# All weights of attention's part staged in the second batch's x memory in slots 0 to 9, and five buffers for v

## The chip, the cores and the metric

The kernel runs on one core of a Trainium2 chip. The metric is the device time of one execution in microseconds (us), median over the runs. The engines of the core work side by side: TensorE (PE, the matmuls, with PEld for its weight loads), VectorE (DVE), ScalarE (ACT), GpSimd (POOL) and SyncE (SP), which here issues every DMA.

## What is computed

Three stages follow each other, all in float32. Attention has 4 batches of 8 heads, 576 positions and 64 columns a head, with a decay term and a causal mask; its output is the input x (2304 tokens, 512 columns) of a first MLP, and that of a second one.

```python
scores = scale * np.matmul(q, k.transpose(0, 1, 3, 2))
cum = np.cumsum(np.log(np.clip(f, 0.0001, 1.0)), axis=-1)
scores = np.where(causal, -1e9, scores + cum[..., :, None] - cum[..., None, :])
attn = softmax(scores)                  # written out in the reference
x = np.matmul(attn, v)                  # then (2304, 512)
h = x @ w_in                            # 512 -> 2048, first MLP
g = np.maximum(h, 0) + alpha * np.minimum(h, 0)
x = g @ w_out                           # 2048 -> 512
out = ((x @ w_a) * (x @ w_b)) @ w_out2  # 512 -> 1536 -> 512, second MLP
```

## The kernel before

Attention goes head by head in 32 slots plus a tail. In slot u PE computes the scores of head u, ACT exponentiates them (line 394), and two slots later `pv` (lines 504 to 520) multiplies the exponentials with v. The exponentials of a head come in three parts, PT_hi, PT_lo and PT_r. Heads 0, 1, 4, 5, 8 and 9 go in whole float32: PE transposes them, and `eng0` in the table `_P` says which engine copies the transposed tile out of PSUM (e4 is the copy of PT_r; lines 249 on ACT, 251 on DVE). The other heads are split into a rounded and a rest part, p_hi, p_lo and p_r (DVE at line 496, POOL at 445), and DMAs transpose them (line 502). For those heads v is split as well: `split_v` (line 347) runs two POOL operations on it. `load_v` (line 338) brings v; before the change there are three v buffers, head u+1 is loaded in slot u, and a buffer is free when `pv` of the head three before it is done. Two finished heads are normalized (xn, xr, lines 532 and 534) and turned by PE (tx, line 548) into the hidden layout, xh and xl (lines 552 and 553), two float32 halves of x.

Beside the slots the first MLP is fed to PE in small portions. It uses 7 blocks of 128 of its 2048 hidden columns in this stage (F1A = 7), so 7 weights of w_in and 7 of w_out, 512 KB each. `fetch` (line 133, on SP) loads a weight, `rounded` splits it by bit arithmetic (ACT at 142, DVE at 144, 145 and 146), and `parts` writes the two halves (ACT at 150, POOL at 151). `ws` in `_P` lists in which slot each of the 14 weights is rounded. `mlp1a` (line 650) computes h with three matmuls for each product (`mm3`, lines 643 to 645), then `leaky`: lu on ACT (637), lt on DVE (638), g on ACT (639), the rest of g on POOL (640); then y, copied by ACT (ys, 685) and stored by SP (686). It starts in slot 10; from that slot on the MLP's matmuls fill the gaps of attention's. Attention's last slot ends at about 365 us; after that come the rest of the first MLP (from 365 on the two kernels have the same code) and the second MLP.

A scheduler orders the instructions of each engine when the kernel is built, and each engine then runs its row of instructions strictly in that order: an instruction that waits holds everything behind it on its engine.

Memory before: while the first MLP has not begun, weights go through a pool `early` with two raw buffers (wr, 4 KB a partition) and one for the rounding (wx); when the MLP begins that pool is closed, and a pool `wstage` with one raw buffer and one wx takes the last three weights, in slots 10 and 11. x has two buffers each for xh and xl, one a batch in turn; the second batch's are first written in slot 11.

Of the kernel before, what the change touches and what calls it, by code (L numbers as in the profile page):

```python
# [10 lines left out]
I32 = mybir.dt.int32  # L11
# [7 lines left out]
B, H, S, D = 4, 8, 576, 64  # L19
# [3 lines left out]
C = DM // 128  # L23
# [21 lines left out]
    rates=[0, 1, 1, 1, 0.8, 1.15, 1.15, 0.95],  # L45
    ws=[0, 1, 2, 3, 4, 5, 6, 7, 8, 9, 9, 10, 10, 11],
    native=10,
    pre=1,
    we=0,
    es=10,  # L50
    eng0={'e0': 'act', 'e2': 'act', 'e3': 'dve', 'e4': 'dve'},
    even0='s3 T p1 s2 vs s0 Q M M M M h3 h2 h0 h1 l1 l2 p0 s1 l0 l3 ri p2 V W M'.split(),
# [37 lines left out]
def decay_attention_then_two_mlps(ctx, tc, q, k, v, f, w_in, w_out, alpha, w_a, w_b, w_o, out):  # L90
# [39 lines left out]
    def fetch(kind, i):  # L130

        raw = mp["stage"].tile([128, C, 128, 2], I32, tag="wraw", name=f"wr_{kind}{i}", bufs=mp["wraw"])
        sp.dma_start(raw.rearrange("p c e t -> p c (e t)"), w_src[kind](i))
        return raw

    def rounded(kind, i, after):

        raw = raws.pop((kind, i), None) or fetch(kind, i)
        low, high = raw[:, :, :, 0], raw[:, :, :, 1]
        x = mp["stage"].tile([128, C, 128], I32, tag="wx", name=f"wx_{kind}{i}", bufs=mp.get("wx"))  # L140
        with tc.issue_after(after) if after is not None else nullcontext():
# [119 lines left out]
    def attention_setup():  # L261
# [35 lines left out]
        for nm in ("nmr", "smr"):  # L297
            ap_[nm] = a.tile([128, 2], F32, tag=nm, name=nm)
        for i in range(3):

            ap_["vs", i] = a.tile([128, 3, NQ, D], F32, tag=f"vs_{i}", name=f"vs_{i}")
            zeros(ap_["vs", i][SR:, :, 4])
# [32 lines left out]
    def load_v(n):  # L335
        b, h = divmod(n, H)
        vs = ap_["vs", n % 3]
        sp.dma_start(vs[:, 0, 0:4], v[b, h, 0:ST].rearrange("(t p) d -> p t d", p=128))
        sp.dma_start(vs[0:SR, 0, 4], v[b, h, ST:])

    def split_v(n):

        if whole(n):
            return
        vs = ap_["vs", n % 3]
        for i in range(2):
            pool.tensor_tensor(vs[:, i + 1], vs[:, i], high(vs[:, i]), op=ALU.subtract)  # L347
# [156 lines left out]
    def pv(u, c):  # L504

        g, j = divmod(u, 2)
        vs = ap_["vs", u % 3]
        if u not in ps_x:
# [67 lines left out]
    def attention():  # L576

        cur = lambda u: 0 <= u < NI
        if LAG == 2:
            load_v(0)  # L580
        warm_up(_P.get("wu", [0, 0])[0], "a")
        stack(0)
# [5 lines left out]
        for u in range(NI + LAG):  # L588
            ap_["u"] = u
            for op in order(u):  # L590
# [28 lines left out]
                elif op == "V":  # L619
                    if cur(u + 3 - LAG):  # L620
                        load_v(u + 3 - LAG)
                elif op == "vs":
# [76 lines left out]
    if True:  # L699
        w1 = lpool(left, "w1", 2 * F1A)  # L700
        xpool = lpool(mid, "x", 2)
        early = ExitStack()
        ap_["early"] = mp["stage"] = lpool(early, "early", 1)
        mp["wraw"] = 2
        decay = decay_sums()
# [31 lines left out]
        def advance():  # L737
            if "g" not in mp:
                assert not raws
                early.close()  # L740
                mp["g"] = [lpool(mid, "g", 1)]
                mp["t"] = lpool(mid, "t", 2)
                mp["stage"] = lpool(mid, "wstage", 1)
                mp["wraw"] = 1
                scores_set(lpool(right, "att3", 1, "right"), 2)
# [10 lines left out]
        for kind, u in att:  # L756
            if kind == "W":
                if u == _P.get("dc", -1):
                    next(decay)
                if u < 0:  # L760
                    raws[todo[0]] = fetch(*todo[0])
                for m in range(_P["ws"].count(u), 0, -1):
                    with tc.high_priority(offset=-_P.get("wp", 0)):
                        if "g" not in mp and (m > 1 or u < NATIVE - 1):
                            raws[todo[1]] = fetch(*todo[1])
                        weight(*todo.pop(0), w1)
                continue
# [15 lines left out]
        mp["stage"] = lpool(right, "wstage2", 2, "right")  # L783
        mp["wx"], mp["wraw"] = 3, 2
        xp = lpool(right, "xb", 2, "right")
# [287 lines left out]
```

## Time and profile before

| | us |
|---|---|
| median of 3 runs (1066.59 to 1068.86) | 1068.8 |
| profiled execution | 1068.39 |
| its span in the trace | 1066.6 |
| around the span | 1.8 |
| PE busy in the span | 1014.8 |
| DVE, ACT, POOL busy in the span | 705.0, 457.4, 413.9 |

The profile page gives the busy time of each engine and the chain of work that ended last. A busy PE is not PE at its full clock: each stretch also has the clock that was granted, as a share of full speed (0.985 over the whole execution). So time is lost in two ways that are read apart, PE's idle time and PE's busy time at a granted clock under 1.

### The profile page before, as it was taken

Reading aid. Unit: us, or ns where it says so; the run is one execution under the profiler, and the core shown is the slowest. Engines: PE = TensorE matmul, PEld = TensorE weight load, DVE = VectorE, ACT = ScalarE, POOL = GpSimd, SP = SyncE. Lnnn points to the kernel's source line nnn. Section 1 sums busy time; section 2 is a strip of 40 time slices with the busy share of each in tenths; the row PEclk is TensorE's granted clock in tenths of the full one; section 3 lists DMA queues with packets and bytes.
Section 4 is the critical chain, followed back from the end, with each engine's and each line's share of the span. In section 5 each row is a group of like instructions: output and inputs, shape, how many; then the busy total and the mean of one; then the engine's idle time right before and its main releaser. Section 6 shows DMA issues by size and latency. Waiting matters only on the chain.

```text
span 1066.6 us, 20175 instructions
## 1 busy us (share of the span) xinstructions
PE 1014.8 (95%) x7485; PEld 959.2 (90%) x7485; DVE 705.0 (66%) x1461; ACT 457.4 (43%) x1035; POOL 413.9 (39%) x413
## 2 busy tenths in 40 slices
PE   5889799998989999999999998999999999999998
PEld 3678689998989999999999998899989999899997
DVE  6889877858767356444456658755986658975553
ACT  4676668758756354333343443322432113221110
POOL 4332623224224155333446866522443224531111
PEclk9999799999989999999999999999999999999999
DMA  6988768977886576756567996726328383353623
GB/s 151 196 190 225 175 142 158 217 159 164 188 194 110 160 246 197 231 190 210 179 231 251 342 366 255 297 96 238 106 93 313 116 315 122 120 209 135 247 89 109
DMA packets 206710, 206.14 MB, mean 193 GB/s; under 512 B 117076, under 2 KB 173908, under 8 KB 206612
## 3 DMA queue, kind: packets, MB, share of 16 engines
q1 hardware_dynamic: 206612, 204.85, 65.2%
q8 instruction: 59, 0.97, 0.4%
q14 instruction: 39, 0.32, 0.1%
HBM read 133.32 MB, written 50.17 MB: 172 GB/s over the span
## 4 chain that ended last, share of the span: by engine, by line
PE 75%; DVE 10%; DMA 6%; issue 3%; POOL 3%; ACT 2%; SPq 0%; POOLq 0%; DVEq 0%; ACTq 0%
PE p L643 7%; PE p L645 7%; PE p L644 7%; PE pv L520 4%; PE o L645 4%; PE o L643 4%; PE o L644 4%; PE ya L643 3%; PE hb L643 3%; PE ya L644 3%; PE hb L645 3%; PE hb L644 3%; PE ya L645 3%; PE y L644 2%; PE y L643 2%
## 5 line engine op out<-in xcount | busy, mean ns | idle before, releaser
L643 PE MATMUL p<-yq,w_h 128*128 128x384 f32 x360 | 121.8, 338 | 2.3 <-DVE lu L1019 1.3
L645 PE MATMUL p<-yq,w_h 128*128 128x384 f32 x360 | 121.3, 337 | 0.0
L644 PE MATMUL p<-yq,w_h 128*128 128x384 f32 x360 | 121.2, 337 | 0.0
L347 POOL TENSOR_TENSOR vs<-vs 128x320 f32<-128x320 f32 x52 | 44.6, 857 | 152.0 <-DMA vs<-in_v 121.2
L394 ACT ACTIVATE s<-s,nm 128x512 f32<-128x512 f32 (+3 forms) x128 | 71.4, 559 | 38.3 <-DVE nm L393 37.1
L643 PE MATMUL o<-w_o,gg 128*128 128x512 f32 x216 | 84.7, 393 | 1.7 <-ACT gg L1000 1.7
L644 PE MATMUL o<-w_o,gg 128*128 128x512 f32 x216 | 84.8, 393 | 0.0
L645 PE MATMUL o<-w_o,gg 128*128 128x512 f32 x216 | 83.2, 393 | 0.0
L1001 POOL TENSOR_TENSOR gg<-tc,gg 128x384 fp32r<-128x384 f32 x36 | 36.6, 1017 | 114.5 <-ACT gg L1000 97.3
L640 POOL TENSOR_TENSOR g<-lt,g 128x288 fp32r<-128x288 f32 x56 | 54.8, 985 | 62.7 <-ACT g L639 62.5
L640 POOL TENSOR_TENSOR gb<-lt,gb 128x384 fp32r<-128x384 f32 x54 | 55.7, 1031 | 59.2 <-ACT gb L639 58.0
L643 PE MATMUL h<-xh,w_in 128*128 128x288 f32 x224 | 67.6, 306 | 8.8 <-DVE lt L638 7.2
L644 PE MATMUL y<-g,w_out 128*128 128x288 f32 x224 | 67.7, 306 | 6.6 <-POOL g L640 6.6
L643 PEld LDWEIGHTS p<-yq,w_h 128*128 128x128 f32 x360 | 67.6, 188 | 6.9 <-DVE lu L1019 1.7
L1001 POOL TENSOR_TENSOR gg<-td,gg 128x384 fp32r<-128x384 f32 x36 | 38.0, 1056 | 89.7 <-ACT gg L1000 83.9
L644 PE MATMUL ya<-gb,w_out 128*128 128x384 f32 x216 | 72.7, 337 | 0.0
L645 PE MATMUL ya<-gb,w_out 128*128 128x384 f32 x216 | 72.5, 336 | 0.0
L643 PE MATMUL ya<-gb,w_out 128*128 128x384 f32 x216 | 71.1, 337 | 1.2 <-DVE yl L842 1.2
L1000 ACT CAST gg<-tc 128x384 fp32r<-128x384 f32 x36 | 18.5, 514 | 125.2 <-DVE tc L999 125.2
L638 DVE SCALAR_TENSOR_TENSOR lt<-lu,nal,hb 128x384 f32<-128x384 f32 x54 | 33.0, 611 | 57.9 <-ACT lu L637 57.9
L644 PEld LDWEIGHTS p<-yq,w_h 128*128 128x128 f32 x360 | 67.6, 188 | 3.7
L643 PE MATMUL y<-g,w_out 128*128 128x288 f32 x224 | 67.6, 312 | 2.8 <-ACT ys L685 2.4
(196 smaller groups left out, 3121.9 us busy)
## 6 DMA issues: line engine op xcount, KB each, us to landing
yq<-yq_d SPq DMA_DIRECT2D x49, 768.0 KB
yq_d<-yhl SPq DMA_DIRECT2D x42, 384.0 KB
yl<-ya_d SPq DMA_DIRECT2D x48, 192.0 KB
po_d<-os SPq DMA_DIRECT2D x36, 256.0 KB
os<-po_d SPq DMA_DIRECT2D x36, 256.0 KB
wr_in<-in_moe_w_in SPq DMA_DIRECT2D x16, 512.0 KB
wr_out<-in_moe_w_out SPq DMA_DIRECT2D x16, 512.0 KB
RK<-in_k SPq DMA_DIRECT2D x44, 144.0 KB
```

The costliest lines, as they stand in the source:

```text
L347: pool.tensor_tensor(vs[:, i + 1], vs[:, i], high(vs[:, i]), op=ALU.subtract)
L394: act.activation(s, s, AF.Exp, bias=nm, scale=-1.0, accum_out=sm)
L520: pe.matmul(o, p, high(vs[:, i, t]), start=start and x == 0, stop=stop and x == len(parts) - 1)
L638: dve.scalar_tensor_tensor(t, u, nal[:, fi:fi + 1], hp[:, :n], op0=ALU.mult, op1=ALU.add)
L640: pool.tensor_tensor(gl, t, f32(gh), op=ALU.subtract)
L643: pe.matmul(o, lh, rh, start=start, stop=False)
L644: pe.matmul(o, lh, rl, start=False, stop=False)
L645: pe.matmul(o, ll, rh, start=False, stop=stop)
L1000: ap_["last"] = act.copy(g[:, 0], o).ins
L1001: pool.tensor_tensor(g[:, 1], o, f32(g[:, 0]), op=ALU.subtract)
```

## The change

`ws` puts all 14 roundings into slots 0 to 9. Their memory comes from the xh and xl tiles of one of x's two buffers, taken under the names home_xh and home_xl: three raw buffers (two in home_xh, one in home_xl) and two for the rounding (in home_xl), used in turn. The first batch of x then takes the other buffer, and the second batch gets this one. Weights are fetched two ahead instead of one. `wstage` is gone. v has five buffers, and slot u loads the v of head u+2 (two loads stand at the start). Six copies of PT_r (`eng0`, e4) go from DVE to ACT.

```diff
-    ws=[0, 1, 2, 3, 4, 5, 6, 7, 8, 9, 9, 10, 10, 11],
+    ws=[0, 1, 1, 2, 3, 3, 4, 5, 5, 6, 7, 7, 8, 9],
-    eng0={'e0': 'act', 'e2': 'act', 'e3': 'dve', 'e4': 'dve'},
+    eng0={'e0': 'act', 'e2': 'act', 'e3': 'dve', 'e4': 'act'},
...
-        raw = mp["stage"].tile([128, C, 128, 2], I32, tag="wraw", name=f"wr_{kind}{i}", bufs=mp["wraw"])
+            raw = mp["home"].pop(0)
+            mp["home"].append(raw)
...
+            x = mp["homex"].pop(0)
+            mp["homex"].append(x)
...
-        for i in range(3):
+        for i in range(5):
             ap_["vs", i] = a.tile([128, 3, NQ, D], F32, tag=f"vs_{i}", name=f"vs_{i}")
...
-        vs = ap_["vs", n % 3]
+        vs = ap_["vs", n % 5]
...
             load_v(0)
+            load_v(1)
...
-                    if cur(u + 3 - LAG):
-                        load_v(u + 3 - LAG)
+                    if cur(u + 4 - LAG):
+                        load_v(u + 4 - LAG)
...
-        mp["wraw"] = 2
+        home = [xpool.tile([128, C * S], I32, tag=x, name=f"home_{x}") for x in ("xh", "xl")]
+        raw_, wx_ = 2 * C * 128, C * 128
+        mp["home"] = [
+            home[j][:, o:o + raw_].rearrange("p (c e t) -> p c e t", c=C, t=2) for j, o in ((0, 0), (0, raw_), (1, 0))
+        ]
+        mp["homex"] = [home[1][:, o:o + wx_].rearrange("p (c e) -> p c e", c=C) for o in (raw_, raw_ + wx_)]
...
-                mp["stage"] = lpool(mid, "wstage", 1)
-                mp["wraw"] = 1
...
-                    raws[todo[0]] = fetch(*todo[0])
-                for m in range(_P["ws"].count(u), 0, -1):
+                    for x in todo[:2]:
+                        raws[x] = fetch(*x)
+                for _ in range(_P["ws"].count(u)):
                     with tc.high_priority(offset=-_P.get("wp", 0)):
-                        if "g" not in mp and (m > 1 or u < NATIVE - 1):
+                        weight(*todo.pop(0), w1)
+                        if len(todo) > 1:
                             raws[todo[1]] = fetch(*todo[1])
-                        weight(*todo.pop(0), w1)
```

Line numbers of the changed kernel are 8 to 12 higher. What it moves is shown at three places.

**Slots 10 and 11, POOL and DVE.** First POOL before. vs_180, vs_176 and vs_178 are the v buffers (of heads 11, 12 and 10 here), g_0 is the first MLP block, w_out are weights, p_11_r is the part p_r of head 11.

```order
L151 TENSOR_TENSOR w_out_1044<-wx_out_1039,w_out_1044 128x512
L151 TENSOR_TENSOR w_out_1194<-wx_out_1189,w_out_1194 128x512
L347 TENSOR_TENSOR vs_180<-vs_180 128x320 x2
L445 TENSOR_SCALAR p_11_r<-sr 128x5x128
L151 TENSOR_TENSOR w_out_1202<-wx_out_1197,w_out_1202 128x512
L347 TENSOR_TENSOR vs_176<-vs_176 128x320 x2
L640 TENSOR_TENSOR g_0_1257<-lt_1280,g_0_1257 128x288
L640 TENSOR_TENSOR g_0_1257<-lt_1318,g_0_1257 128x288
L640 TENSOR_TENSOR g_0_1257<-lt_1369,g_0_1257 128x288
L640 TENSOR_TENSOR g_0_1257<-lt_1428,g_0_1257 128x288
L151 TENSOR_TENSOR w_out_1395<-wx_out_1390,w_out_1395 128x512
```

The same place on POOL in the changed kernel (vs_182, vs_184 and vs_186 are the further buffers, of heads 12, 13 and 14):

```order
L159 TENSOR_TENSOR w_out_929<-home_xl,w_out_929 128x512
L355 TENSOR_TENSOR vs_180<-vs_180 128x320 x2
L159 TENSOR_TENSOR w_out_1065<-home_xl,w_out_1065 128x512
L355 TENSOR_TENSOR vs_182<-vs_182 128x320 x2
L159 TENSOR_TENSOR w_out_1212<-home_xl,w_out_1212 128x512
L649 TENSOR_TENSOR g_0_1264<-lt_1287,g_0_1264 128x288
L649 TENSOR_TENSOR g_0_1264<-lt_1325,g_0_1264 128x288
L649 TENSOR_TENSOR g_0_1264<-lt_1376,g_0_1264 128x288
L649 TENSOR_TENSOR g_0_1264<-lt_1415,g_0_1264 128x288
L453 TENSOR_SCALAR p_11_r<-sr 128x5x128
L355 TENSOR_TENSOR vs_184<-vs_184 128x320 x2
L649 TENSOR_TENSOR g_0_1264<-lt_1463,g_0_1264 128x288
```

The last weights now stand ahead of the first g, the split of head 12 too, and p_11_r stands behind four of the g.

DVE before, around the first lt, the operation that feeds the first g:

```order
L393 ISA nm_164 128x1
L416 TENSOR_SCALAR smr<-smr 128x1
L496 SCALAR_TENSOR_TENSOR p_11_r<-sr,p_11_r 128x5x128
L496 SCALAR_TENSOR_TENSOR p_11_hi<-s_163,p_11_hi 128x7x128
L417 RECIPROCAL rir_167<-smr 128x1
L416 TENSOR_SCALAR sm_165<-sm_165 128x4
L553 TENSOR_TENSOR xl_1573<-tx_0_1574,xh_1572 128x256
L417 RECIPROCAL ri_166<-sm_165 128x4
L553 TENSOR_TENSOR xl_1573<-tx_1_1579,xh_1572 128x320
L496 SCALAR_TENSOR_TENSOR p_11_lo<-s_163,p_11_lo 128x3x128
L638 SCALAR_TENSOR_TENSOR lt_1280<-lu_1281,nal,h_0_0_1258 128x288
L638 SCALAR_TENSOR_TENSOR lt_1318<-lu_1319,nal,h_0_1_1286 128x288
```

And in the changed kernel:

```order
L401 ISA s_152,nm_153<-sc_3_1312,maskz 128x512
L401 ISA nm_153 128x1
L647 SCALAR_TENSOR_TENSOR lt_1287<-lu_1288,nal,h_0_0_1265 128x288
L647 SCALAR_TENSOR_TENSOR lt_1325<-lu_1326,nal,h_0_1_1293 128x288
L401 ISA s_152,nm_153<-sc_1_1346,maskz 128x256
L401 ISA nm_153 128x1
L259 COPY PT_9_lo<-tp_0_0_1352 128x384
L504 SCALAR_TENSOR_TENSOR p_10_hi<-s_152,p_10_hi 128x7x128
L424 TENSOR_SCALAR sm_154<-sm_154 128x4
L647 SCALAR_TENSOR_TENSOR lt_1376<-lu_1377,nal,h_0_2_1331 128x288
L504 SCALAR_TENSOR_TENSOR p_10_lo<-s_152,p_10_lo 128x3x128
```

The first lt stood behind the rest scores and p_11 of head 11; it now stands among the work of heads 9 and 10.

**Heads 6 and 7, SP.** Weight loads (L133, in the change L137), transposes (L502, in the change L510), v loads (L338, in the change L346) and the other loads share this one row. Before:

```order
L502 DMA_TRANSPOSE PT_hi<-p_6_hi 128x14x128
L502 DMA_TRANSPOSE PT_lo<-p_6_lo 128x6x128
L338 DMA vs_180<-in_v 128x4x64
L339 DMA vs_180<-in_v 64x64
L502 DMA_TRANSPOSE PT_r<-p_7_r 128x10x128
L133 DMA wr_out_899<-in_moe_w_out 128x1024
L502 DMA_TRANSPOSE PT_hi<-p_7_hi 128x14x128
L502 DMA_TRANSPOSE PT_lo<-p_7_lo 128x6x128
L338 DMA vs_176<-in_v 128x4x64
L339 DMA vs_176<-in_v 64x64
```

In the changed kernel, the same heads:

```order
L137 DMA home_xh<-in_moe_w_out 128x1024
L332 DMA RK_150<-in_k 64x576
L334 DMA RQ_149<-in_q 64x576
L510 DMA_TRANSPOSE PT_hi<-p_6_hi 128x14x128
L346 DMA vs_178<-in_v 128x4x64
L347 DMA vs_178<-in_v 64x64
L137 DMA home_xh<-in_moe_w_out 128x1024
L332 DMA RK_163<-in_k 64x576
L510 DMA_TRANSPOSE PT_lo<-p_6_lo 128x6x128
L336 DMA RQ_162<-in_q 64x512
L510 DMA_TRANSPOSE PT_r<-p_7_r 128x10x128
L510 DMA_TRANSPOSE PT_hi<-p_7_hi 128x14x128
```

The weight load stands ahead of PT_hi of head 6 and again ahead of PT_lo, where it stood between PT_r and PT_hi of head 7; the v load of a head stands one head earlier against the transposes.

**The start, ACT.** The first weight's rounding (wx_in, in the change home_xl) beside the work of head 0. Before:

```order
L394 ACTIVATE s_150,sm_152<-s_150,nm_151 128x256
L249 COPY PT_0_hi<-tp_2_0_248 128x384
L413 ACTIVATE sr,smr<-sr,nmr 128x576
L142 ACTIVATE wx_in_229<-wr_in_207 128x512
L394 ACTIVATE s_163,sm_165<-s_163,nm_164 128x512
L249 COPY PT_0_lo<-tp_0_0_269 128x384
```

In the changed kernel:

```order
L402 ACTIVATE s_152,sm_154<-s_152,nm_153 128x256
L150 ACTIVATE home_xl<-home_xh 128x512
L257 COPY PT_0_hi<-tp_2_0_254 128x384
L421 ACTIVATE sr,smr<-sr,nmr 128x576
L150 ACTIVATE home_xl<-home_xh 128x512
L402 ACTIVATE s_165,sm_167<-s_165,nm_166 128x512
L257 COPY PT_0_lo<-tp_0_0_275 128x384
```

The first operation on a weight went from behind the copy of PT_0_hi and the exponential sr to ahead of both, and that of the second weight stands right behind.

## Rows read from the trace of the kernel before

**Rows 1.** Windows: start:end, us, busy of PE, PEld, DVE, ACT, POOL, clock, DMA share, GB/s.

```profile
13.00:105.00 92.00, 85.39 (x757) 70.62 (x757) 78.91 (x246) 61.75 (x159) 25.30 (x25) 0.98 0.88 202
105.00:144.00 39.00, 28.54 (x287) 26.78 (x286) 32.32 (x68) 25.68 (x60) 21.41 (x19) 0.82 0.69 159
144.00:365.00 221.00, 212.12 (x2652) 205.34 (x2652) 152.20 (x424) 145.68 (x367) 67.89 (x80) 0.97 0.77 163
365.00:1066.60 701.60, 688.72 (x3792) 656.46 (x3792) 434.23 (x712) 220.19 (x445) 288.84 (x260) 1.00 0.59 205
```

**Rows 2.** Waits of PE in 105 to 365: us in total, times, longest.

```profile
PE h L643 <- DVE lt L638: 7.2, 2, 5.9
PE y L644 <- POOL g L640: 6.6, 4, 2.8
PE y L643 <- ACT ys L685: 2.4, 1, 2.4
```

**Rows 3.** The chain of waits, 100 to 145: start, us, what.

```profile
102.58 3.79 DMA vs<-in_v
...
108.02 0.70 POOL p_r L445
...
110.62 1.52 DVE p_hi L496
...
116.25 3.74 DMA RK<-in_k
...
129.57 4.05 DMA wr_out<-in_moe_w_out
```

**Rows 4.** Windows behind PE's waits, two of the four at low clock.

```profile
114.47:120.20 5.73, 5.73 (x24) 5.73 (x25) 5.18 (x8) 2.65 (x7) 3.81 (x3) 0.50 1.04 235
...
305.20:311.00 5.80, 5.79 (x23) 5.58 (x24) 3.99 (x10) 3.89 (x10) 3.23 (x4) 0.50 0.91 187
```

**Rows 5.** Timeline of POOL: start, us, what, [idle before <-releaser].

```profile
212.70 0.72 POOL L347 TENSOR_TENSOR vs<-vs 128x320 f32<-128x320 f32 x1 [6.21 <-DMA vs<-in_v]
...
302.90 1.51 POOL L347 TENSOR_TENSOR vs<-vs 128x320 f32<-128x320 f32 x2 [2.44 <-DMA vs<-in_v]
```

**Rows 6.** Waits of POOL in 105 to 365.

```profile
POOL vs L347 <- DMA vs<-in_v: 99.8, 17, 12.6
```

**Rows 7.** Operations in 13 to 105: count | busy, mean ns | idle before.

```profile
L146 DVE SCALAR_TENSOR_TENSOR wx_in<-wr_in,wx_in 128x512 int32<-128x512 int32 x7 | 4.8, 683 | 0.0
...
L142 ACT ACTIVATE wx_in<-wr_in 128x512 f32<-128x512 f32 x7 | 4.7, 676 | 5.5 <-POOL w_in L151 5.1 <-DMA wr_in<-in_moe_w_in 0.5
...
L150 ACT CAST w_in<-wx_in 128x512 fp32r<-128x512 f32 x7 | 4.3, 616 | 3.1 <-DVE wx_in L146 3.1
...
L144 DVE TENSOR_SCALAR wx_in<-wx_in 128x512 int32<-128x512 int32 x7 | 3.0, 427 | 3.1 <-ACT wx_in L142 3.1
...
L251 DVE COPY PT_r<-tp 128x384 f32<-128x384 f32 x3 | 1.7, 557 | 0.1
...
L251 DVE COPY PT_r<-tp 128x256 f32<-128x256 f32 x3 | 1.3, 417 | 0.0
```

**Rows 8.** Timeline of ACT, the first operation on a weight.

```profile
20.15 0.48 ACT L249 COPY PT_hi<-tp 128x384 f32<-128x384 f32 x1 [1.26 <-PE tp L453]
...
21.85 0.68 ACT L142 ACTIVATE wx_in<-wr_in 128x512 f32<-128x512 f32 x1 [0.45 <-DMA wr_in<-in_moe_w_in]
```

**Rows 9.** Timeline of PE, its two long waits in the first ten heads.

```profile
40.52 0.65 PE L520 MATMUL pv<-vs,PT_hi 128*128 128x64 bf16 x16 [2.85 <-DMA PT_hi<-p_hi]
...
74.03 1.16 PE L520 MATMUL pv<-vs,PT_hi 128*128 128x64 bf16 x33 [2.51 <-DMA PT_hi<-p_hi]
```

**Rows 10.** The chain of waits, 30 to 86: two transposes, issue to use.

```profile
44.00 5.84 DMA PT_hi<-p_hi
...
79.08 5.59 DMA PT_hi<-p_hi
```

**Rows 11.** Timeline of SP, the issue of a weight load.

```profile
78.39 0.59 SPq L133 DMA_DIRECT2D wr_out<-in_moe_w_out  x1
```

## What the change does to the time: the prediction

> **What bounds the kernel now.** I read the times by stage first [rows 1]: from each line, the stretch less the busy time of PE is PE's idle time, and the column behind the five engines is the granted clock. From 365 us on PE is busy for 688.72 of 701.60 us at clock 1.00, and the code there stays as it is, so nothing is to be had there. From 13 to 105 (the first ten heads, with the weights) PE idles 92.00 - 85.39 = 6.6 us at 0.98. From 105 to 144 it idles 39.00 - 28.54 = 10.5 us at 0.82, and from 144 to 365 it idles 221.00 - 212.12 = 8.9 us at 0.97. PE sets the end in all of them, and what can be gained lies in these idle times and in the busy time at a low clock behind them: 28.54 x 0.18 = 5.1 us in the second stretch and 212.12 x 0.03 = 6.4 us in the third.
>
> Then I ask what PE waits for [rows 2]. The long ones are the MLP's operations: lt on DVE (7.2 us, of which 5.9 in one wait), the rest of g on POOL (6.6 us in four waits) and ys on ACT (2.4 us). None of the three is slow in itself, so the question is what stands ahead of them. The chain of waits [rows 3] tells it for the first of them: the load of v lands after 3.79 us, POOL splits v and only then writes p_r of head 11 (108.02), DVE's p_r and p_hi wait for that, and lt stands behind them in DVE's row. Later the same chain goes over a k load (3.74 us) and a load of w_out (4.05 us) whose rounding holds DVE and ACT until ys. In the third stretch POOL's timeline shows the same in two places [rows 5]: POOL stands 6.21 and 2.44 us idle for v with the split, and the next operation is the rest of g for which PE waits. Over 105 to 365 POOL waits for v in 17 places, 99.8 us in all [rows 6]; most of that costs nothing, since only where a g is queued behind it does PE notice. Behind such a wait the granted clock is 0.50, the lower level of 1.2 GHz, for some 5.8 us [rows 4]: PE had stood idle 5.9 us before the first of these stretches and 2.8 before the second. Half of 5.73 is lost there, 2.9 us, on top of the wait.
>
> **The change part by part.** All sums start at the profiled execution, 1068.4 us (span 1066.6 and 1.8 around it), 0.4 under the median.
>
> *Slots 10 and 11 (105 to 144).* The change takes the last weights out of there and brings v one slot earlier. In the new order lt stands before head 11's p_r and p_hi on DVE, and on POOL the first g stands ahead of p_11_r; the first MLP block no longer passes through head 11's rest at all. The upper bound is all the idle time and all the lost clock, 10.5 + 5.1 = 15.6. The lower bound is what the chain puts down to the two transfers alone, v and w_out, 3.79 + 4.05 = 7.8 [rows 3]. What stays on the chain is the k load, 3.74, with nothing in the change that brings it sooner; 15.6 - 3.7 = 11.9, so I take -12.
>
> *Slots 12 to 31 (144 to 365).* A v load now has a slot more, so POOL should find v there. The waits of PE that go with it are those on g, 6.6, and on lt beside the one long wait, 7.2 - 5.9 = 1.3; together 7.9 [rows 2]. The upper bound is the idle time and the clock, 8.9 + 6.4 = 15.3; the lower is half of the 7.9, 4, if the other half has a second late input (ACT's g, say) and no clock comes back. I take -8: the clock that returns and the waits that stay about cancel. The two additional buffers cost memory alone.
>
> *The first ten heads (13 to 105).* Here three more weights are rounded than before. DVE pays 3 x (0.427 + 2 x 0.683) = 5.4 us and is spared six copies, 1.7 + 1.3 = 3.0 [rows 7]: +2.4. ACT pays 3 x (0.676 + 0.616) = 3.9 and six copies of about 0.48 [rows 7, 8], together some 6.8; it is busy for 61.75 of 92 us [rows 1], and that hides it. POOL is busy for 25.30 of them, which hides three more operations there. DVE, at 78.91 of 92, is nearer its limit: I take half, 1.2 of the 2.4. The three loads are 1.57 MB; at the 202 GB/s of the stretch that is 7.8 us if the DMA engines were full, but their share is 0.88 and leaves 92 x 0.12 = 11 us: I take 0.4, upper bound 7.8 (DVE's 2.4 would lie inside it). At the start ACT's first operation on a weight now stands ahead of the copy of PT_0_hi and the exponential behind it. Before, ACT had done both of those and then still waited 0.45 us for the weight [rows 8]. Now it waits for the same arrival with the copy (0.48 us, at 20.15) behind it: the copy comes 21.85 + 0.68 - 20.15 = 2.4 us later, and about 3.5 if the second load that goes out beside it delays the first by its share. PE needs the copy for `pv` of head 0 and has scores of the next head to do in the meantime, so I take a little over half of the 2.4: 1.4, with 0 to 3.5 as bounds. Sum: +1.2 + 0.4 + 1.4 = +3. The upper bound is 7.8 + 3.5 = +11.3; below nothing it can go as far as PE's idle time, -6.6, since the earlier v and the fetch two ahead also relieve POOL and SP here.
>
> Sum: 1068.4 - 12 - 8 + 3 = 1051.4. The ends of all terms: 1068.4 - 15.6 - 15.3 - 6.6 = 1030.9 and 1068.4 - 7.8 - 4 + 11.3 = 1067.9.
>
> **The rivals.**
>
> *Next in line.* The waits for v vanish and others take their place: the k load, ACT's g, the DVE row. For: the chain already has the k load next to v [rows 3]. Against: POOL's 6.21 us [rows 5] stand directly ahead of the g that PE wants. Then only the transfers of slots 10 and 11 are gained and 1 us later: 1068.4 - 7.8 - 1 + 3 = 1062.6.
>
> *All of it.* The idle time of slots 10 to 31 goes with the clock of slots 10 and 11, and the two waits of the first ten heads, 2.85 + 2.51 = 5.4 us [rows 9], with it: 1068.4 - 15.6 - 8.9 - 5.4 = 1038.5. For: the new order of SP issues v well ahead of the transposes. Against: those two waits are for transposes by DMA, which the change doesn't hasten.
>
> *Slower: transposes behind weight loads.* SP's new order brings weight loads ahead of transposes of heads 2, 3, 6 and 7 (two of the places stand above for heads 6 and 7). If a transpose has to let the 512 KB go first, it lands 0.52 MB / 202 GB/s = 2.6 us later, and PE already waits for transposes in that stretch [rows 9]. Four times 2.6, with 3.5 at the start and the gains at their lower bounds, 11.8, is 1068.4 + 10.4 + 3.5 - 11.8 = 1070.5; with a stretch of low clock behind each, 2.9 us [rows 4], it is 1082; I price it at 1076. It decides from (11.8 - 3.5) / 4 = 2.1 us for each of the four, clock included. Against: the transpose issued at 79.08 stood right behind a weight load (78.39) and took 5.59 us until its use; the one issued at 44.00 without a load right ahead took 5.84 [rows 10, 11]. So the trace shows no such delay. The Trainium skill ("DMA: Bandwidth & Descriptors", "Two DMAs through the same engine are not ordered") says that within one queue of one DMA engine descriptors start in order but are pipelined. By that rule the transposes do queue behind the weights, and this rival would be the rule's own result; the two durations just given don't bear it out in full.
>
> *It doesn't do what it says.* SP's row is in order, and a v load that stands early in it can still be issued late if a load ahead waits for its buffer. Then POOL waits for v as before, and only w_out's 4.05 comes off: 1068.4 - 4.05 + 3 = 1067.4.
>
> **How the numbers follow.** Forecast 0.60, next in line 0.15, all of it 0.10, transposes behind weights 0.09, no earlier v 0.06. The range reaches from 1039 to 1066: it leaves out the slower rival, the one without earlier v and about half of "all of it", together 0.2. A measurement of this kernel can tell about 0.2%, 2.1 us, from no change. Faster by more than that are the first three, 0.85; the last one is the same, 0.06; slower 0.09.
>
> **What would show it.** In the profile after, POOL's wait for v in 105 to 365 should be far under 99.8 us; the chain after 105 should hold neither v nor w_out; PE's 5.9 us wait for lt should be gone and the clock in slots 10 and 11 near 1. The waits on g should be under 3 us in all. The first matmul of the MLP should come no more than some 3 us later than before; waits of PE for transposes over 5 us each would speak for the slower rival. A v that POOL still waits for with a g behind it would show the forecast wrong, and so would an unchanged wait of g on ACT.

## The result, and the profile after

The changed kernel takes 1056.8 us (median of 4 runs, 1056.07 to 1059.55) against 1068.8 before: 0.9895 of the time, 95% interval 0.9871 to 0.9919. The profiled execution took 1056.55 us with a span of 1054.8. The forecast was 1051.4 with a range of 1039 to 1066.

To see where the 11.8 us between the two spans went, both traces are cut at the same work. Two marks are taken: the fourth tx, with which PE turns heads 6 and 7 (90.94 us before, 103.21 after), and the seventh (171.50 and 166.80). The last cut is the first matmul after attention (365.82 and 354.42). Some of the expectations below speak of the first matmul of the MLP instead of the fourth tx; it stands 2.5 us ahead of it in both kernels (88.48 and 100.76). Windows of before (start:end, us, busy time and count of PE, PEld, DVE, ACT and POOL, granted clock, DMA share, GB/s):

```profile
13.18:90.94 77.76, 71.33 (x642) 56.71 (x643) 65.48 (x208) 51.95 (x137) 20.65 (x20) 0.98 0.87 194
90.94:171.50 80.56, 69.82 (x711) 67.38 (x710) 66.42 (x159) 56.41 (x135) 35.46 (x34) 0.89 0.75 173
171.50:365.82 194.32, 184.90 (x2345) 178.64 (x2344) 132.12 (x371) 124.99 (x313) 58.35 (x69) 0.97 0.78 164
```

The same three pieces of the changed kernel:

```profile
13.45:103.21 89.76, 74.55 (x641) 59.21 (x642) 77.26 (x220) 60.55 (x154) 33.72 (x31) 0.94 0.92 196
103.21:166.80 63.59, 63.59 (x711) 62.47 (x710) 52.61 (x141) 49.17 (x125) 25.68 (x29) 1.00 0.83 184
166.80:354.42 187.62, 181.89 (x2346) 175.98 (x2344) 131.30 (x371) 124.87 (x314) 55.33 (x65) 0.99 0.80 168
```

PE's matmul counts agree to one in each piece (642 and 641, 711 and 711, 2345 and 2346), so these pieces hold the same work, and PE's time in each is its busy time and the rest, idle time:

| piece | before | after | difference | of it idle | of it busy (clock) |
|---|---|---|---|---|---|
| start to the fourth tx | 90.94 | 103.21 | +12.3 | 6.4 to 15.2 | 71.3 to 74.6 |
| fourth to seventh tx | 80.56 | 63.59 | -17.0 | 10.7 to 0.0 | 69.8 to 63.6 |
| seventh tx to the end of attention | 194.32 | 187.62 | -6.7 | 9.4 to 5.7 | 184.9 to 181.9 |
| after attention | 700.8 | 700.4 | -0.4 | | |

So the change gains 24 us in attention's later slots and gives half of it back in the first ten heads. In the middle piece PE is busy all the time at clock 1.00. What is left of PE's waits from 105 us on (us in total, times, longest), to be read against [rows 2]:

```profile
PE y L653 <- POOL g L649: 2.6, 2, 2.4
PE h L652 <- DVE xl L561: 1.1, 1, 1.1
PE y L652 <- DVE lt L647: 0.9, 1, 0.9
PE h L652 <- DVE lt L647: 0.6, 1, 0.6
PE h L652 <- ACT ys L694: 0.5, 1, 0.5
```

The waits on the rest of g went from 6.6 to 2.6 us, that of 5.9 for lt and that of 2.4 for ys are gone. POOL's own waits in the same stretch:

```profile
POOL g L649 <- ACT g L648: 73.5, 28, 19.3
POOL vs L355 <- DMA vs<-in_v: 42.5, 14, 8.3
```

It waits for v 42.5 us instead of 99.8 [rows 6], and longer for ACT's g, 73.5 us instead of 40.0; PE's waits on g fell all the same.

The loss ahead of the fourth tx is in PE's timeline, four of its eight waits of over 0.4 us there:

```profile
23.96 0.70 PE L385 MATMUL sc<-N 128*128 128x256 f32 x2 [2.03 <-ACT PT_hi L257]
...
43.87 0.82 PE L528 MATMUL pv<-vs,PT_hi 128*128 128x64 bf16 x12 [3.79 <-DMA PT_hi<-p_hi]
...
73.77 0.51 PE L385 MATMUL scr<-N 128*128 128x288 f32 x1 [3.77 <-ACT PT_hi L257]
...
84.59 0.61 PE L528 MATMUL pv<-vs,PT_hi 128*128 128x64 bf16 x11 [2.46 <-DMA PT_hi<-p_hi]
```

Before, the two long ones were 2.85 and 2.51 us [rows 9]. After three of these waits the clock of the next 5 us is 0.67 to 0.68 in the mean (windows as above; the last line stands behind the longest wait of slots 12 to 31, 2.36 us):

```profile
43.87:49.00 5.13, 5.13 (x60) 4.39 (x61) 4.52 (x12) 4.68 (x13) 3.08 (x2) 0.67 0.92 230
73.77:79.00 5.23, 5.23 (x18) 3.66 (x18) 4.93 (x14) 5.23 (x12) 0.21 (x1) 0.67 0.61 179
84.59:90.00 5.41, 5.17 (x47) 4.01 (x47) 5.32 (x13) 2.52 (x9) 3.42 (x3) 0.68 1.19 159
295.05:300.00 4.95, 4.95 (x25) 4.76 (x25) 3.70 (x11) 4.12 (x11) 2.42 (x3) 0.66 1.01 207
```

The same windows behind the two long waits of the kernel before, 2.51 and 2.85 us:

```profile
74.03:79.00 4.97, 4.60 (x64) 3.44 (x64) 4.88 (x14) 4.12 (x12) 1.69 (x2) 1.00 0.62 129
40.52:45.60 5.08, 4.99 (x58) 3.71 (x59) 4.99 (x14) 3.29 (x9) 0.30 (x1) 0.66 0.75 159
```

A third of some 5.2 us busy is 1.7 us, three times in the changed kernel and once in the kernel before, and PE's busy time for the piece grew by 3.2 us. With 8.8 us more of idle time, and 0.3 at the start, that makes the 12.3.

DVE did more in this piece, too: it is busy 77.3 us instead of 65.5. Up to the fourth tx the changed kernel has begun all 14 weights on DVE, the kernel before nine, and each of the three operations on a weight takes longer. Here is the last of the three (the windows of the first piece, with the busy time and count of this operation alone, L146 before and L154 after):

```profile
13.18:90.94 77.76, 5.46 (x8) 0.98 0.87 194
13.45:103.21 89.76, 11.18 (x14) 0.94 0.92 196
```

All three together are 29.7 us instead of 15.3.

### The profile page after: what moved, and what is told of

It is laid out like the page before. It is cut to its first block, busy times and chain, and to the rows that moved or that the text cites. A ratio compares the mean times of both kernels' runs of the same rounds, so it can differ in the third digit from the quotient of the medians.

```text
span 1054.8 us, 20173 instructions
## 1 busy us (share of the span) xinstructions
PE 1008.6 (96%) x7485; PEld 954.1 (90%) x7485; DVE 701.7 (67%) x1455; ACT 458.7 (43%) x1041; POOL 414.5 (39%) x415
## 4 chain that ended last, share of the span: by engine, by line
PE 74%; DVE 10%; DMA 7%; issue 3%; POOL 3%; ACT 2%; SPq 1%; POOLq 0%; DVEq 0%; ACTq 0%
PE p L652 7%; PE p L654 7%; PE p L653 7%; PE pv L528 5%; PE o L652 4%; PE o L653 4%; PE o L654 4%; PE hb L652 3%; PE ya L652 3%; PE hb L654 3%; PE ya L653 3%; PE hb L653 3%; PE ya L654 3%; PE h L652 2%; PE h L653 2%
## 5 line engine op out<-in xcount | busy, mean ns | idle before, releaser
L355 POOL TENSOR_TENSOR vs<-vs 128x320 f32<-128x320 f32 x52 | 42.6, 818 | 87.5 <-DMA vs<-in_v 63.6
L653 PE MATMUL y<-g,w_out 128*128 128x288 f32 x224 | 66.5, 300 | 2.6 <-POOL g L649 2.6
L401 DVE CUSTOM_DVE_ANT_0 s<-sc,maskz 128x512 f32<-128x512 f32 (+3 forms) x128 | 60.5, 483 | 11.1 <-PE sc L389 7.9
```

What stands on the lines that cost most here:

```text
L401: dve.tensor_tensor_reduce(s, o, m, -0.125, 3.0e38, ALU.add, ALU.min, nm)
L653: pe.matmul(o, lh, rl, start=False, stop=False)
```

## The experiments

The table puts all runs side by side. Ratios are against the kernel before in the same session; the marks are from each run's trace. "Rounding" is the number of buffers for the rounding (wx in the kernel before), and "last weight" is when POOL began the second half of the fourteenth weight.

| run | raw | rounding | v | ratio, 95% interval | last weight | fourth tx | fourth to seventh | seventh to end |
|---|---|---|---|---|---|---|---|---|
| before | 2, then 1 | 1 | 3 | | 138.9 | 90.9 | 80.6 | 194.3 |
| after | 3 | 2 | 5 | 0.9895 (0.9871 to 0.9919) | 104.5 | 103.2 | 63.6 | 187.6 |
| v3_early_weights | 3 | 2 | 3 | 0.9980 (0.9963 to 0.9996) | 104.8 | 103.8 | 65.4 | 193.3 |
| v5_late_weights | 3 | 2 | 5 | 0.9915 (0.9888 to 0.9942) | 98.8 | 101.8 | 67.8 | 189.3 |
| v3_late_weights | 3 | 2 | 3 | 0.9939 (0.9918 to 0.9960) | 104.3 | 101.3 | 64.2 | 193.8 |
| first_weight_slot_1 | 3 | 2 | 5 | 0.9881 (0.9860 to 0.9901) | 104.2 | 102.0 | 65.0 | 187.0 |
| raw2 | 2 | 2 | 5 | 0.9903 (0.9885 to 0.9921) | 105.9 | 103.8 | 64.5 | 186.8 |
| half_load | 3 | 2 | 5 | 0.9885 (0.9867 to 0.9903) | 101.1 | 98.9 | 66.2 | 188.2 |
| no_low_bits | 3 | 2 | 5 | 0.9900 (0.9885 to 0.9916) | 91.2 | 101.8 | 64.8 | 188.2 |
| raw2_later_weights | 2 | 2 | 5 | 0.9892 (0.9872 to 0.9913) | 102.8 | 100.7 | 64.7 | 187.4 |
| six_copies_on_dve | 3 | 2 | 5 | 0.9915 (0.9882 to 0.9947) | 98.9 | 101.8 | 64.9 | 187.3 |
| old_staging_v5 | 2 | 1 | 5 | 0.9951 (0.9931 to 0.9971) | 147.3 | 92.8 | 79.5 | 185.8 |
| one_rounding_buffer | 2 | 1 | 5 | 0.9943 (0.9923 to 0.9963) | 148.7 | 94.6 | 77.5 | 186.4 |
| old_staging_two_rounding | 2 | 2 | 5 | 0.9888 (0.9863 to 0.9913) | 109.5 | 101.8 | 66.5 | 190.0 |

Each edit below is against the changed kernel unless it says otherwise. The scheduler makes a new order for each, so rows move beside the edited ones, too.

**v undone, the weights' slots undone, both undone.**

v3_early_weights:

```diff
-        for i in range(5):
+        for i in range(3):
...
-        vs = ap_["vs", n % 5]
+        vs = ap_["vs", n % 3]
...
-            load_v(1)
...
-                    if cur(u + 4 - LAG):
-                        load_v(u + 4 - LAG)
+                    if cur(u + 3 - LAG):
+                        load_v(u + 3 - LAG)
```

> The changed kernel with v as before: three buffers, head u+1 loaded in slot u. The weights stay early. Theory A (both parts carry the gain; v gives the 7 us by which slots 12 to 31 became shorter, and a part of the 16.6 of slots 10 and 11): 1064 to 1068 us, POOL waits for v in 105 to 365 near 100 us again, and PE waits for g behind it return. Rival B (the gain comes from the weights leaving slots 10 and 11 alone): 1056 to 1058. Rival C (the gain is v's alone): 1069 or more, since the first ten heads would still pay 12 us.

v5_late_weights:

```diff
-    ws=[0, 1, 1, 2, 3, 3, 4, 5, 5, 6, 7, 7, 8, 9],
+    ws=[0, 1, 2, 3, 4, 5, 6, 7, 8, 9, 9, 10, 10, 10],
```

> The changed kernel with the roundings of the weights as in the kernel before, one a slot (two in slot 9, three in slot 10, since slot 11 is taken by the second batch's x). Five v buffers stay. Theory A (rounding early costs some 12 us in the first ten heads and gains some 8 to 12 in slots 10 and 11): the first matmul of the MLP near 89 us instead of 100.8, but PE waits in slots 10 and 11 of 6 to 10 us; total 1053 to 1058. Rival B (the weights' leaving of slots 10 and 11 carries the gain): 1064 to 1068. Rival C (v carries it, the early weights are a loss): 1045 to 1050.

v3_late_weights holds both edits (of the v part the first lines alone are shown again):

```diff
-    ws=[0, 1, 1, 2, 3, 3, 4, 5, 5, 6, 7, 7, 8, 9],
+    ws=[0, 1, 2, 3, 4, 5, 6, 7, 8, 9, 9, 10, 10, 10],
...
-        for i in range(5):
+        for i in range(3):
...
```

> Both undone: three v buffers and roundings one a slot; what is left of the change is the staging in x's memory, the fetch two ahead and the six copies on ACT. Theory A: 1065 to 1070, the same as before. If the staging or the six copies matter by themselves: below 1063 or above 1072.

Measured: 1066.0, 1060.4 and 1062.4 us. Both parts carry a gain, as theory A had it, but not where it put them. The v part is read from the last piece: 193.3 and 193.8 us with three buffers, as before (194.3), and 187.6 and 189.3 with five. So v gives 4.5 to 5.7 us in slots 15 to 31; over all runs this piece takes 185.8 to 190.0 us with five buffers and 193.3 to 194.3 with three. The waits show it, more clearly with early weights than with late ones, where PE's waits for g are 5.4 us with five buffers and 7.2 with three; in v3_early_weights PE's waits for g (first line: of PE) and POOL's for v (second fence) are back:

```profile
PE y L652 <- POOL g L648: 8.9, 6, 2.8
```

```profile
POOL vs L355 <- DMA vs<-in_v: 103.6, 17, 11.4
```

with POOL idle for v ahead of a g at the same place as in the kernel before [rows 5]:

```profile
211.48 0.72 POOL L355 TENSOR_TENSOR vs<-vs 128x320 f32<-128x320 f32 x1 [6.32 <-DMA vs<-in_v]
```

The weights' slots did nothing that was expected of them. With the roundings late in the table the fourth tx stayed at 101 to 102 us, and the last weight was done at 98.8 and 104.3, as early as in the changed kernel. The table only says when a rounding enters the program; the scheduler then places it, and the runs with one rounding buffer below show that the buffers decide how early. In v3_late_weights nothing but the staging in x's memory with its fetch two ahead and the six copies was left, and the first ten heads were still 10 us longer and the middle piece 16 us shorter than before. The two early-or-late pairs differ in total by +3.6 us with v's three buffers and -3.6 with five, mostly ahead of the seventh tx; differences of some 3 us that change sign I take for an effect of the order and not of the slots, which no run shows.

**The first weight later.** 

```diff
-    ws=[0, 1, 1, 2, 3, 3, 4, 5, 5, 6, 7, 7, 8, 9],
+    ws=[1, 1, 1, 2, 3, 3, 4, 5, 5, 6, 7, 7, 8, 9],
```

> The changed kernel with the first weight rounded in slot 1 instead of slot 0 (three in slot 1). Theory A (ACT's 3.9 us wait for the first weight holds the copy of PT_0_hi and costs PE 2.0 us): the 2.0 us wait of PE at 22 us is gone and the total is 1054 to 1056. Rival (PE's time in the first ten heads is set by the DMA engines, so the start doesn't matter): 1056 to 1058, with the wait moved to a later place.

Measured: 1056.2 us, no difference from the changed kernel. The edit missed its aim: ACT's row still has the weight ahead of the copy of PT_0_hi, and it still waits:

```profile
22.57 0.66 ACT L150 ACTIVATE home_xl<-home_xh 128x512 f32<-128x512 f32 x1 [3.79 <-DMA home_xh<-in_moe_w_in]
```

PE's wait for that copy stays as well, 1.91 us after the 2.03 of the changed kernel. So this run tells nothing on what it would bring to take the wait away.

**Raw buffers, bytes, DVE operations.** Four runs on what the first ten heads pay for.

raw2:

```diff
-            home[j][:, o:o + raw_].rearrange("p (c e t) -> p c e t", c=C, t=2) for j, o in ((0, 0), (0, raw_), (1, 0))
+            home[j][:, o:o + raw_].rearrange("p (c e t) -> p c e t", c=C, t=2) for j, o in ((0, 0), (0, raw_))
```

> The changed kernel with two raw weight buffers instead of three, as many as before the change; all else as changed. Theory A2 (the 12 us lost in the first ten heads come from the third raw buffer: SP issues weight loads earlier, the DMA engines are full from 30 to 75 us, and q, k and the transposes land later): the first matmul of the MLP near 91 to 95 us instead of 100.8, DMA share from 30 to 75 back to about 0.9, total 1047 to 1052. Rival D (DVE and ACT, with the weights' bit arithmetic, are the limit there): the first matmul of the MLP stays at 99 to 101, total 1055 to 1059.

half_load (the part that is not loaded is set to zero once at the start, by POOL):

```diff
-        sp.dma_start(raw.rearrange("p c e t -> p c (e t)"), w_src[kind](i))
+        if "stage" in mp:
+            sp.dma_start(raw.rearrange("p c e t -> p c (e t)"), w_src[kind](i))
+        else:
+            sp.dma_start(raw.rearrange("p c e t -> p c (e t)")[:, 0:2], w_src[kind](i)[:, 0:2])
...
+        for r in mp["home"]:
+            pool.memset(r[:, 2:4], 0)
```

> The changed kernel with only half of each of the 14 weights loaded (256 KB instead of 512; the other half of the memory is zero, so the output is wrong); all operations on DVE, ACT and POOL remain. That takes 3.7 MB off the DMA engines ahead of 105 us, some 18 us of their time at 200 GB/s. Theory A2 (DMA is the limit of the first ten heads): first matmul of the MLP at 86 to 92 us, total 1042 to 1048. Rival D (DVE and ACT are the limit): 98 to 101, total 1054 to 1057.

no_low_bits:

```diff
-        dve.scalar_tensor_tensor(x, low, 29, x, op0=ALU.logical_shift_right, op1=ALU.bitwise_or)
+        if "stage" in mp:
+            dve.scalar_tensor_tensor(x, low, 29, x, op0=ALU.logical_shift_right, op1=ALU.bitwise_or)
```

> The changed kernel without the last of the three DVE operations on each of the 14 weights (the low bits are left out, so the output is less exact): 14 x 0.68 = 9.6 us less of DVE's work in the first ten heads; all loads remain. Rival D (DVE is the limit there): first matmul of the MLP at 92 to 95 us, total 1047 to 1051. Theory A2 (DMA): 98 to 101, total 1054 to 1057.

raw2_later_weights is raw2 with

```diff
-    ws=[0, 1, 1, 2, 3, 3, 4, 5, 5, 6, 7, 7, 8, 9],
+    ws=[0, 1, 2, 3, 4, 5, 6, 7, 7, 8, 8, 9, 9, 10],
```

> Two raw buffers, and the roundings one a slot up to slot 6 and then two a slot, the last in slot 10. Theory A2: the first ten heads as in the run with two raw buffers or 1 to 3 us better, slots 10 and 11 without long waits as long as the last weight is done before the first y: 1045 to 1052. Rival (rounding late costs slots 10 and 11 again): 1055 to 1060.

Measured: 1057.2, 1055.5, 1057.0 and 1055.9 us. All four agree with the changed kernel within their intervals, and theory A2 and rival D both fall: two raw buffers leave the fourth tx at 103.8, and 9.6 us of DVE's work less leave it at 101.8 with the weights themselves done sooner (91.2). In that run DVE is busy for 68.1 us of the first piece instead of 77.3, and PE idles 16.2 us in it, 14.7 of them in two waits for transposes:

```profile
45.91 2.05 PE L529 MATMUL pv<-vs,PT_hi 128*128 128x64 bf16 x35 [7.17 <-DMA PT_hi<-p_hi]
84.26 2.05 PE L529 MATMUL pv<-vs,PT_hi 128*128 128x64 bf16 x35 [7.53 <-DMA PT_hi<-p_hi]
```

The 1.4 us that it gains at the mark say little: first_weight_slot_1 and six_copies_on_dve, without any effect on the total that can be measured, stand at 102.0 and 101.8 as well. Half the bytes give the most, 98.9, that is 4.3 us sooner. Of these 2.4 don't come from the bytes: in this run's order PE's first matmul stands at 11.04 us instead of 13.45, and the first weight load is issued only at 17.44.

```profile
11.04 4.17 PE L388 MATMUL sc<-N 128*128 128x512 f32 x8 [11.04 <-DMA N<-rows]
```

So 1.9 of the 12.3 us are left for the bytes. The DMA share of that stretch falls to 0.71 and still PE idles 85.91 - 74.08 = 11.8 us in it:

```profile
13.00:98.91 85.91, 74.08 (x641) 59.44 (x639) 76.83 (x220) 59.54 (x151) 31.61 (x33) 0.90 0.71 166
98.91:165.07 66.16, 64.06 (x710) 62.57 (x710) 53.54 (x143) 49.76 (x126) 26.88 (x29) 1.00 0.76 177
```

**The copies and the rounding buffer.**

old_staging_v5 holds these edits, the six copies back on DVE and the table of v5_late_weights:

```diff
-            home[j][:, o:o + raw_].rearrange("p (c e t) -> p c e t", c=C, t=2) for j, o in ((0, 0), (0, raw_), (1, 0))
+            home[j][:, o:o + raw_].rearrange("p (c e t) -> p c e t", c=C, t=2) for j, o in ((0, 0), (0, raw_))
-        mp["homex"] = [home[1][:, o:o + wx_].rearrange("p (c e) -> p c e", c=C) for o in (raw_, raw_ + wx_)]
+        mp["homex"] = [home[1][:, o:o + wx_].rearrange("p (c e) -> p c e", c=C) for o in (raw_,)]
...
-                    for x in todo[:2]:
+                    for x in todo[:1]:
...
-                        weight(*todo.pop(0), w1)
                         if len(todo) > 1:
                             raws[todo[1]] = fetch(*todo[1])
+                        weight(*todo.pop(0), w1)
```

> The changed kernel with the staging of before inside x's memory: two raw buffers, one for the rounding, one weight fetched ahead and its load put ahead of the rounding before it, the six copies back on DVE, and roundings one a slot (three in slot 10). What stays of the change is v (five buffers, loads a slot earlier) and that no weight is left in slot 11. Up to now every version lost 8 to 13 us up to the turn of heads 6 and 7 (PE's fourth tx, at 90.9 us before and 99 to 104 in all versions), with the DMA volume halved too. Theory E (that loss comes from the new staging and the order it makes, not from v): fourth tx at 90 to 94 us, total 1046 to 1054. Rival F (the loss comes with the earlier v loads): fourth tx at 99 or later, total 1056 to 1062.

six_copies_on_dve:

```diff
-    eng0={'e0': 'act', 'e2': 'act', 'e3': 'dve', 'e4': 'act'},
+    eng0={'e0': 'act', 'e2': 'act', 'e3': 'dve', 'e4': 'dve'},
```

> The changed kernel with the six copies of PT_r back on DVE, nothing else undone. Theory G (the copies on ACT hold the score tiles in PSUM longer and cost PE its waits on ACT's PT copies): fourth tx at 95 to 98 us, total 1050 to 1053. Rival (they are a relief of DVE): fourth tx at 104 or later, total 1057 to 1060. Theory E: no change, 1055 to 1058.

one_rounding_buffer (early slots, copies on ACT, and of old_staging_v5 the buffers with the load ahead of the rounding):

```diff
-            home[j][:, o:o + raw_].rearrange("p (c e t) -> p c e t", c=C, t=2) for j, o in ((0, 0), (0, raw_), (1, 0))
+            home[j][:, o:o + raw_].rearrange("p (c e t) -> p c e t", c=C, t=2) for j, o in ((0, 0), (0, raw_))
-        mp["homex"] = [home[1][:, o:o + wx_].rearrange("p (c e) -> p c e", c=C) for o in (raw_, raw_ + wx_)]
+        mp["homex"] = [home[1][:, o:o + wx_].rearrange("p (c e) -> p c e", c=C) for o in (raw_,)]
...
-                    for x in todo[:2]:
+                    for x in todo[:1]:
...
-                        weight(*todo.pop(0), w1)
                         if len(todo) > 1:
                             raws[todo[1]] = fetch(*todo[1])
+                        weight(*todo.pop(0), w1)
```

> The changed kernel with the buffers of before (two raw, one for the rounding, the load put ahead of the rounding before it), early roundings, the six copies on ACT and v as changed. Theory E, if the buffers make the order that costs: fourth tx at 92 to 97 us, total 1048 to 1053. If it is the early rounding in the slots that costs: fourth tx at 99 to 104, total 1055 to 1060.

Measured: 1063.0, 1059.1 and 1061.8 us. Theory E was right on the fourth tx and wrong on the total. With one rounding buffer the fourth tx is back at 92.8 and 94.6 us, with early slots too, so the slots are not the cause, and v's earlier loads aren't either. But the time isn't gained: the fourth to seventh tx take 79.5 and 77.5 us again. POOL's timeline shows what is late. The last weight in the changed kernel:

```profile
104.46 1.29 POOL L159 TENSOR_TENSOR w_out<-home_xl,w_out 128x512 fp32r<-128x512 f32 x1
```

and in old_staging_v5 and one_rounding_buffer, behind ACT's first half of the same weight:

```profile
147.26 1.27 POOL L159 TENSOR_TENSOR w_out<-home_xl,w_out 128x512 fp32r<-128x512 f32 x1 [4.88 <-ACT w_out L158]
```

```profile
148.73 1.41 POOL L159 TENSOR_TENSOR w_out<-home_xl,w_out 128x512 fp32r<-128x512 f32 x1 [3.09 <-ACT w_out L158]
```

With one rounding buffer each weight has to pass through ACT, three DVE operations, ACT and POOL before the next may begin, and the fourteenth is done 40 us later. PE waits in that piece mostly for nm, which DVE writes with the masked scores, and in DVE's row the late weights' operations still stand: 5.8 of the 10.2 us that PE idles there in old_staging_v5. The longest of these waits:

```profile
141.90 0.44 PE L388 MATMUL sc<-U,T 128*128 128x128 f32 x1 [3.22 <-DVE nm L401]
```

The six copies on DVE make no difference that can be measured: the interval, 0.9882 to 0.9947, holds the 0.9895 of the changed kernel.

That leaves one edit to try by itself, the second rounding buffer. old_staging_two_rounding against old_staging_v5:

```diff
-        mp["homex"] = [home[1][:, o:o + wx_].rearrange("p (c e) -> p c e", c=C) for o in (raw_,)]
+        mp["homex"] = [home[1][:, o:o + wx_].rearrange("p (c e) -> p c e", c=C) for o in (raw_, raw_ + wx_)]
```

> The run with the old staging and five v buffers (1063.0 us; two raw buffers, one for the rounding), with a second rounding buffer and nothing else. Theory H (the second rounding buffer decides when the weights are done, whatever the slots in the table say: with one, the last weight is done at 147 to 149 us in both runs that had one, with two, at 93 to 106 in all that had two): the last weight done by 106 us, the fourth tx at 98 to 104 instead of 92.8, the seventh tx at 164 to 169 instead of 172.3, total 1054 to 1059. Rival J (the slots in the table or the third raw buffer decide it): the last weight after 125 us, seventh tx at 170 or later, total 1060 to 1065.

Measured: 1058.5 us, ratio 0.9888 (0.9863 to 0.9913) against 0.9951 (0.9931 to 0.9971) without it. The last weight comes at 109.5, a little later than expected and far from rival J's 125:

```profile
109.54 1.29 POOL L159 TENSOR_TENSOR w_out<-home_xl,w_out 128x512 fp32r<-128x512 f32 x1 [3.75 <-ACT w_out L158]
```

The three pieces of old_staging_v5, and then with the second rounding buffer:

```profile
13.30:92.82 79.52, 71.54 (x642) 57.24 (x642) 64.90 (x209) 54.10 (x140) 21.99 (x25) 0.98 0.83 193
92.82:172.32 79.50, 69.29 (x711) 64.68 (x710) 66.61 (x162) 54.37 (x134) 34.48 (x35) 0.96 0.85 182
172.32:358.16 185.84, 180.36 (x2345) 174.55 (x2343) 131.21 (x369) 124.56 (x313) 54.41 (x65) 1.00 0.78 167
```

```profile
13.48:101.79 88.31, 72.57 (x641) 58.29 (x642) 76.35 (x221) 57.42 (x144) 29.05 (x28) 0.96 0.92 198
101.79:168.24 66.45, 64.35 (x711) 62.60 (x710) 55.74 (x147) 50.65 (x127) 28.27 (x30) 1.00 0.76 176
168.24:358.24 190.00, 183.51 (x2346) 177.40 (x2344) 130.89 (x371) 125.05 (x316) 55.38 (x65) 0.98 0.80 167
```

One buffer moves the first piece by +9.0 us (92.82 to 101.79) and the second by -13.0 (79.50 to 66.45), with the same matmuls in each. That is the trade of the whole change ahead of slot 15, +12.3 and -17.0. Theory H stands. What the trade is worth in total these two traces don't show: the third piece is 4.2 us longer in the second one, both end attention at 358.2 us, and the profiled execution of old_staging_two_rounding, 1061.75 us, is the longest of its four. The gain stands in the medians, 1063.0 and 1058.5, and in the two intervals, which don't touch. No version of the twelve is faster than the changed kernel by more than their intervals.

## Why the prediction held, and where it did not

**Slots 10 and 11: right that it goes, wrong on what moves it, and too small.** The step had -12 with 15.6 as its upper bound; the piece around it, which reaches on to slot 14, gave -17.0, all of its idle time (10.7) and all of its lost clock (6.2). The -12 left the k load, 3.74 us [rows 3], on the chain as it was, and that fell too. No run took the k load apart from the weights, so that the weight loads ahead of it on SP held it is an argument, not a finding. The cause is, however, not what the text leaned on, the slots of the table and v: with three v buffers and late slots the piece still shrinks to 64.2 us, with one rounding buffer it stays at 77 to 80. It was the second rounding buffer, which stands in the account of the change and which the sum never priced.

**Slots 12 to 31: right.** Forecast -8 (bounds -4 and -15.3), measured -6.7 (the piece begins in slot 15), of which 4.5 to 5.7 go with the v buffers in two pairs of runs. The mechanism is as put: POOL's wait for v with a g behind it (99.8 to 42.5 us in all), and the clock behind (0.97 to 0.99). The longest wait that is left, PE's 2.36 us at 295.05, is still of that kind: POOL waits for v and then does the g.

```profile
293.53 0.72 POOL L355 TENSOR_TENSOR vs<-vs 128x320 f32<-128x320 f32 x1 [2.77 <-DMA vs<-in_v]
```

**The first ten heads: the term that was mis-sized.** Forecast +3, bounds -6.6 and +11.3, measured +12.3, outside its own bounds. Each piece of the sum treated the extra weights as volume on an engine with room to spare: DVE half of 2.4, DMA 0.4, ACT nothing. The volume itself was too small: the sum counted three more weights up to a fixed time, 5.4 us on DVE, where up to the same work, the fourth tx, five more are begun and DVE's three operations take 14.3 us more. Yet DVE's time alone isn't the answer either, since the run with 9.2 us less of it in this piece moved the mark by 1.4. The start was sized well (1.4 forecast; PE waits 2.03 us at 23.96 for the copy behind ACT's 3.92 us wait for the first weight). PE's long waits are for things that come through several queues: ACT at 71.32 waits 4.45 us for a q load, and the copy of PT_hi for which PE waits (73.77) stands behind that in ACT's row:

```profile
22.88 0.66 ACT L150 ACTIVATE home_xl<-home_xh 128x512 f32<-128x512 f32 x1 [3.92 <-DMA home_xh<-in_moe_w_in]
...
71.32 0.72 ACT L371 CAST T<-RQ 128x640 fp32r<-128x640 f32 x1 [4.45 <-DMA RQ<-in_q]
```

Having one rounding buffer gave some 9 us of it back (94.6 and 92.8 us at the mark), halving the bytes 1.9 and leaving out a DVE operation at most 1.4. So faster weights cost the heads these microseconds, and neither the bytes nor DVE's time explains most of them. That the weights take their share of SP's row, the DMA engines, DVE and ACT all at once is the reading that fits, but it isn't shown: no run changed the pace of the weights without also changing the order, and what each queue takes stays open.

**The rivals.** "All of it" came true for the middle piece alone. The slower rival, transposes behind weight loads, didn't come true in the total, but its mechanism is not out. Two transposes on the chain of the changed kernel, issue to use, the second, a PT_lo, issued 1 us behind a weight load:

```profile
38.62 5.20 DMA PT_hi<-p_hi
...
84.20 6.51 DMA PT_lo<-p_lo
```

The two PT_hi of before took 5.84 and 5.59 [rows 10], so 5.20 shows no delay. The 6.51 can't be held against them, since a PT_lo has 6 blocks and a PT_hi 14. The same tiles in old_staging_v5, with no weight load issued in the 7 us ahead of them, and then a PT_r in old_staging_two_rounding and one in v3_late_weights, issued 1.2 and 1.0 us behind one:

```profile
43.09 3.43 DMA PT_r<-p_r
72.33 4.09 DMA PT_lo<-p_lo
```

```profile
83.64 6.30 DMA PT_r<-p_r
```

```profile
46.52 4.43 DMA PT_r<-p_r
```

Tile for tile that is 2.4, 2.9 and 1.0 us more behind a weight load, around the 2.1 from which the rival would have decided. These are single transfers among other loads, and what a weight load ahead costs a transpose stays open. PE's longest wait for a transpose in the changed kernel, 3.79 us, is under the 5 that were to speak for the rival; in no_low_bits two are over it (7.17 and 7.53). PE's waits for transposes up to the fourth tx went from 5.7 to 8.3 us with the change, and from 5.3 to 10.0 with the second rounding buffer alone. That the total came out faster is due to the gains, which were 24 us instead of the 11.8 of this rival's sum. The Trainium skill's rule ("DMA: Bandwidth & Descriptors", "Two DMAs through the same engine are not ordered") allows such a delay, and these rows agree with it in part.

**The signs named beforehand.** POOL's wait for v far under 99.8: yes, 42.5, though some of it still has a g behind it. The 5.9 us wait for lt gone and the clock near 1: yes. Waits on g under 3 us: yes, 2.6. No v and no w_out on the chain after 105: w_out is gone, two loads of v (2.07 and 2.86 us) are left. The wait of g on ACT, which was not to stay as it was, rose from 40.0 to 73.5 without harm, so it was no sign. The first matmul of the MLP at most 3 us later: no, 12.3 us later. This sign tells that the total, 1056.8 for 1051.4, fits in part by luck: 9 us more lost in the first ten heads than forecast met 5 more gained in slots 10 to 14.

## What to carry to other kernels

Here the number of rounding buffers set the pace of the weights, and not the slot in which a table asks for the work; so price each buffer that a change adds, and look in the built order for where the work went. A side job that is made faster can cost the main work more than its volume on any one engine: count what it does up to the same piece of work, not up to the same time, and ask which queues it shares with the transfers that the main work waits for. When a gain is smaller than the waits that vanished, cut both traces at the same work and check it by instruction counts: here that turned one difference of 12 us into +12, -17 and -7.

## What was not expected of the hardware

What a wait of PE costs behind it can't be read from its length. Waits of 2.36 to 3.79 us in the changed kernel were followed by some 5 us at 0.66 to 0.68 in the mean (the four windows above), and so was one of 2.85 in the kernel before; one of 2.51 there was followed by 5 us at 1.00, one of 2.8 by 5.8 us at 0.50 [rows 4]. So a wait of 2.4 to 2.9 us brought nothing more, 1.7 or 2.9 us more. And taking 256 KB off each of fourteen loads, 3.7 MB in all, shortened the way from PE's first matmul to the fourth tx by 1.9 us only, though the DMA share ahead of it had been 0.92.
